# Writes of tokens to the experts' table that do not wait for one another

## The chip, the cores and the metric

The kernel runs on one core of one Trainium2 chip. The metric is the device time of one execution in microseconds (us). The core has four compute engines with an instruction stream each, TensorE (PE in the profile), VectorE (DVE), ScalarE (ACT) and GpSimd (POOL), and SyncE (SP), which here issues most transfers. Each engine takes its own instructions in order: an instruction that waits holds up all that stand behind it on that engine.

## What is computed

Three operators follow one another: a gated linear attention, a bilinear feed-forward layer over all 3072 tokens, and a layer of eight experts in which each token goes to one expert alone.

```python
for t in range(S):                                   # attention, per head
    state = alpha[:, :, t, :, None] * state + np.einsum('bhd,bhe->bhde', k[:, :, t], v[:, :, t])
    y[:, :, t] = np.einsum('bhd,bhde->bhe', q[:, :, t], state)
...
x = ((x @ w_a) * (x @ w_b)) @ w_out                  # 3072 x 384, d_ff 1536
...
logits = x @ w_gate + modality_bias[modality_id]     # 8 experts
e_idx = np.argmax(logits, axis=1)
gate_w = probs[np.arange(N), e_idx]
for e in range(E):
    mask = e_idx == e
    h = np.maximum(x[mask] @ w1[e], 0.0)
    out[mask] = gate_w[mask, None] * (h @ w2[e])
```

## The kernel before

**Windows.** The tokens are worked on in eight windows of 384, numbered 0 to 7. For one window, `Attention` makes the attention's output, `moe` runs the feed-forward layer on it (PE lines L625 and L616, with the copies `asb`, `gh` on ACT and the products `g`, `gl` on DVE), and `route` decides each token's expert. In one turn of the main loop, three windows are in work at once: the attention of window w+1, `moe` of window w and `route` of window w-1. A scheduler that works on estimated times puts their instructions into an order for each engine, once, when the program is built; some stretches are ordered by hand.

**The table.** `route` gives each token a row of its own in a table in HBM, `tab_d`, which has a stretch of rows for each expert. A row is 8 bytes: the token's number and its weight. A window has three blocks of 128 tokens, and so `route` ends with three indirect writes issued by POOL (L732), each of 128 rows to places that are only known when the kernel runs. I call such a write a put; there are 24. Since the places are not known beforehand, the framework lets each put wait until the put before it has landed, whatever its window, except where it is told that two have nothing to do with each other. Before the change it was told so for the last window alone (`route` of window 7, which passes a list `puts`).

**Experts.** The expert layer works in slots of 256 tokens of one expert. `Slot.index` reads a slot's 256 rows of the table (L920, into the tile `rt`; `rte` for the first three slots), from a row whose number SP loads from a register tile with `value_load` (L918). `Slot.load` fetches the slot's tokens by their numbers (POOL, L931, `xg`) and the expert's weights (SP, L944 and L948, `w1r` and `w2r`); `value_load` at L940 gives the expert. `Slot.split` divides the weights into a high and a low part (ACT L968 and DVE or POOL L969). The first three slots are filled from windows 0 to 6 and begin while `moe` of window 7 still runs; they read the table once `route` of window 6 has written it. In that stretch the order on DVE and ACT is written by hand, so that ACT's copies of the first slot's weights (`w0he<-w1re`) stand between its copies for `moe`.

**POOL's other work.** Between the puts POOL multiplies the attention's queries by the running products of the gates (`qt`, L392), and the state by them (`state`, L437). `qt` at L392 reads the tile `at`, of which there is one buffer alone; DVE's next transposition into `at` (L358) therefore waits for it. Behind that transposition stand on DVE, among other things, the guards of later loads of `alpha` (`amin` and `amax` from the tile `late`, loaded by SP at L276 into buffers that DVE has to free first) and the product `g` of `moe` (L632), for which PE waits.

Of the kernel before, what the change touches and what calls it, by code (L numbers as in the profile page):

```python
# [28 lines left out]
RATIO = 3  # L29
# [8 lines left out]
MIX = 5, 2, 2  # L38
# [6 lines left out]
def gla_moe_kernel(ctx, tc, q, k, v, alpha, w_a, w_b, w_out, modality_id, w_gate, modality_bias, w1, w2, out):  # L45
# [9 lines left out]
    NW = N // WIN  # L55
# [92 lines left out]
    ap = m2 = fold = None  # L148
# [512 lines left out]
            cols += [t[:, j * DM : (j + 1) * DM] for j in range(n)]  # L661
        return cols

    def route(w, pool, gate=None, puts=None):


        L = work.tile([P, CPW, E], F32, tag="L", name=f"L{w}")
# [62 lines left out]
        for t in range(CPW):  # L730
            i = w * CPW + t
            put = nc.gpsimd.indirect_dma_start(  # L732
                out=tab_d[:, :],
                out_offset=bass.IndirectOffsetOnAxis(ap=posi[:, t : t + 1], axis=0),
                in_=rec[:, i, :],
                in_offset=None,
                bounds_check=E * CAP - 1,
                oob_is_err=False,
            )
            if puts is not None:  # L740
                if puts:
                    tc.declare_no_dep(put.ins, group=puts[0].ins.name, reason="every token has a row of its own")
                puts.append(put)
                tc.add_to_no_dep_group(puts[0].ins.name, put.ins)
        yield

    def run(*gens):
# [30 lines left out]
    def small(name, shape, dt=F32):  # L778
        return m2.tile(shape, dt, bufs=1, name=name)
# [375 lines left out]
    def pipeline(y_d=None):  # L1155
        nonlocal ap, m2, fold, starts
        nc.vector.tensor_copy(base, eoff)
        with tc.tile_pool(name="att", bufs=1) as ap:
            if y_d is None:
                starts = ap.tile([P, NPAIR * P1], F32, name="starts")  # L1160
# [13 lines left out]
            if y_d is None:  # L1174
# [36 lines left out]
                for w in range(1, NW - 1):  # L1211
                    if w == 1:
                        with tc.issue_after(newest["mm"].ins):
                            turn_gate()
                        gate = gate_columns("gate", ap, 2, tag="cv", bufs=4)
                    att = Attention(w + 1)
                    run((after_first(att.steps()) if w == 1 else att.steps(), RATIO), (moe(w), 1), (route(w - 1, ap, gate if w > 2 else None), 1))
            else:
                for r in range(NF // 2):
                    load_weights(r)  # L1220
# [2 lines left out]
                for w in range(NW - 1):  # L1223
                    x_from(w, y_d)
                    run((moe(w), 1))
                    if w < NW - 2:
                        run((route(w, ap), 1))
                x_from(NW - 1, y_d)
        with tc.tile_pool(name="m2", bufs=2) as m2:
            fold = small("fold", [P, TINY])  # L1230
            nc.vector.tensor_reduce(fold, ident.rearrange("p (j c) -> p c j", c=TINY), axis=AX.X, op=ALU.add)
            last = moe(NW - 1)
            gate = gate_columns("last", m2, 4, tag="wr", bufs=6) if y_d is None else None
            run((islice(last, 1), 1))
            early = []
            run((islice(last, MIX[0]), 1), (behind(chain(route(NW - 2, m2, gate), early_table(early))), 2))
            slots = [Slot(f"e{i}", "e", i, 2, (NW - 1) * WIN) for i in range(NEARLY)]
            for s_ in slots:
                s_.index()
            for s_ in slots[:2]:  # L1240
                s_.load()
            run((islice(last, MIX[1]), 1))
            if y_d is None:
                run((behind(spans()), 1))
            with tc.manual_schedule(engines=VECS):
                run((last, 1), (slots[0].split(), SPLIT), (behind(pause(MIX[2], slots[0].rows())), 1))

            big, tiny = [("l", i, 2) for i in range(NSB)], [("r", XSMALL + i, 1) for i in range(NTINY + XTINY)]
            order, rest = big[:NBIG], [big[NBIG:], [("r", i, 1) for i in range(XSMALL)], tiny[NTINY:]]
            riders = {}  # L1250
            if y_d is None:
                riders = {RIDE[n]: Tiny(f"t{n}", *tiny[n][:2], N) for n in range(NTINY)}
            else:
                order, rest = big + rest[1] + tiny, []
            slots += [Slot(f"l{n}", *o, N) for n, o in enumerate(order)]
            with nullcontext() if rest else tc.manual_schedule(engines={EN.SP}):
                puts = []
                go(slots, 1, (route(NW - 1, m2, puts=puts), early[0], puts), riders)
        return rest

    def pause(n, steps):
        for _ in range(n):
# [3 lines left out]
    def go(slots, ready, more=None, riders={}):  # L1266
# [19 lines left out]
        for i, s in enumerate(slots):  # L1286
# [5 lines left out]
            with tc.manual_schedule(engines=VECS):  # L1292
# [4 lines left out]
                if i + 1 < len(slots):  # L1297
# [4 lines left out]
                    if wait:  # L1302
                        run((aside, 1))
                        slots[i + 2].index()
                        for put in more[2]:
                            tc.add_manual_dep(
                                slots[i + 2].taken.ins,
                                put.ins.name,
                                mybir.DependencyInfo(mybir.DependencyClass.Sync, mybir.DependencyReason.DATA),
                                reason="rows of the table",  # L1310
                            )
                        slots[i + 2].load()
                    run((steps, 1), (nxt, 2), (islice(aside, 4), 1), (beside, 1))
                else:
# [91 lines left out]
```

## Time and profile before

| | |
|---|---|
| median of 3 runs | 896.39 us (895.86 to 898.45) |
| the profiled execution | 897.17 us, of which the span of the profile is 895.2 us |
| PE busy | 840.8 us, 94% of the span |
| DVE, ACT, POOL busy | 71%, 33%, 22% of the span |
| puts (L732 on POOL) | 24, busy 24.2 us; idle time of POOL just before them 135.7 us, of which 67.0 us until an earlier put had landed |

PE is busy for nearly the whole span, so that time can only be won where PE stands still or runs below its full clock. The profile gives both: the idle time ahead of an instruction with what ended it, and the granted clock of a stretch.

The columns of a stretch's row in the section below are its bounds and length, the busy time and count of PE, PEld, DVE, ACT and POOL, then PE's granted clock (1.00 is 2.4 GHz), the DMA engines' share and GB/s.

### The profile page before, as it was taken

To read this page: it belongs to the slowest core of one execution; us is meant where nothing else is said; L and a number is where in the kernel's file an instruction comes from. 1 tells how busy PE (TensorE), PEld (TensorE's weight loads), DVE (VectorE), ACT (ScalarE), POOL (GpSimd) and SP (SyncE) were. 2 spreads that over 40 slices of the span, in tenths; PEclk is the share of its full clock that TensorE was granted. 3 is DMA by queue.
4 is the path that set the end of the run, shared out by engine and by line. 5 is a ranking of instruction groups with operands and counts; after the bars stand their busy time and mean duration, and the time that the engine had idled before them with its cause. 6 is when DMAs were issued, how large, how long until landed. Compare 5 with 4: busy or idle time off the path is not lost.

```text
span 895.2 us, 16751 instructions
## 1 busy us (share of the span) xinstructions
PE 840.8 (94%) x6220; PEld 786.0 (88%) x6220; DVE 636.0 (71%) x1457; ACT 292.1 (33%) x681; POOL 199.5 (22%) x273
## 2 busy tenths in 40 slices
PE   7888889988997999999999999999699999999995
PEld 6677789978996999989899998999699999998994
DVE  7699889964595788499698676366369876775751
ACT  2223332212221222212122122122265555565541
POOL 5011101120011101011100100000425565455431
PEclk9889999998998999999999999999899999999998
DMA  9999846332234214023220000210580988695810
GB/s 170 200 197 199 181 123 207 93 62 68 63 77 74 81 28 106 27 63 96 41 78 10 1 28 1 71 28 1 202 299 24 361 289 310 191 358 186 281 60 22
DMA packets 124928, 110.98 MB, mean 124 GB/s; under 512 B 55759, under 2 KB 104051, under 8 KB 124836
## 3 DMA queue, kind: packets, MB, share of 16 engines
q1 hardware_dynamic: 114548, 99.00, 40.7%
q0 software_dynamic: 4032, 9.62, 3.1%
q10 hardware_dynamic: 6256, 1.19, 1.1%
q8 instruction: 51, 0.84, 0.4%
q14 instruction: 41, 0.34, 0.1%
HBM read 100.10 MB, written 9.82 MB: 123 GB/s over the span
## 4 chain that ended last, share of the span: by engine, by line
PE 65%; DVE 12%; DMA 10%; issue 6%; SPq 3%; POOL 2%; ACT 2%; POOLq 0%; DVEq 0%; ACTq 0%
PE ab L625 24%; PE px L616 12%; PE hl L1056 8%; PE pol L1004 8%; DMA wa<-in_moe_w_a 3%; PE he L1056 2%; PE s L404 2%; PE poe L1004 2%; DMA wb<-in_moe_w_b 2%; DMA tab_d<-rec,posi 2%; PE u L493 1%; DVE g L632 1%; DMA raw_a<-in_alpha 1%; SPq L162 1%; DVE at L358 1%
## 5 line engine op out<-in xcount | busy, mean ns | idle before, releaser
L625 PE MATMUL ab<-xh,pb 128*128 128x384 f32 x576 | 168.8, 346 | 16.3 <-DVE g L632 16.3
L625 PE MATMUL ab<-xh,pa 128*128 128x384 f32 x576 | 167.4, 344 | 9.7 <-ACT asb L630 7.3
L616 PE MATMUL px<-po,gh 128*128 128x384 f32 x576 | 139.5, 342 | 3.4 <-ACT gh L634 3.1
L634 ACT ACTIVATE gh<-g 128x384 fp32r<-128x384 f32 x96 | 50.3, 524 | 240.4 <-DVE g L632 234.4
L625 PEld LDWEIGHTS ab<-xh,pb 128*128 128x128 f32 x576 | 107.5, 191 | 21.4 <-DVE g L632 18.3
L625 PEld LDWEIGHTS ab<-xh,pa 128*128 128x128 f32 x576 | 106.2, 190 | 14.0 <-ACT asb L630 7.9
L632 DVE TENSOR_TENSOR g<-ab,asb 128x384 f32<-128x384 f32 x96 | 53.0, 552 | 81.5 <-PE ab L625 75.6
L616 PEld LDWEIGHTS px<-po,gh 128*128 128x128 f32 x576 | 104.3, 191 | 5.5 <-ACT gh L634 4.1
L625 PE MATMUL ab<-xl,pb 128*128 128x384 f32 x288 | 98.0, 340 | 0.0
L625 PE MATMUL ab<-xl,pa 128*128 128x384 f32 x288 | 97.4, 338 | 0.0
L630 ACT ACTIVATE asb<-ab 128x384 f32<-128x384 f32 x96 | 47.0, 490 | 147.8 <-PE ab L625 147.5
L616 PE MATMUL px<-po,gl 128*128 128x384 f32 x288 | 87.0, 341 | 0.0
L638 DVE TENSOR_TENSOR gl<-g,gh 128x384 fp32r<-128x384 f32 x96 | 56.2, 586 | 21.6 <-ACT gh L634 21.3
L392 POOL TENSOR_TENSOR qt<-qt,at 128x512 f32<-128x512 f32 x18 | 22.3, 1237 | 220.8 <-DVE qt L358 168.3
L1061 DVE SCALAR_TENSOR_TENSOR hll<-hl,hhl 128x256 fp32r<-128x256 f32 x72 | 30.3, 421 | 54.1 <-ACT hhl L1059 53.7
L671 DVE SCALAR_TENSOR_TENSOR junk<-xr,gate 128x384 bf16<-128x384 f32 x96 | 54.0, 562 | 4.8 <-ACT xr L648 3.2
L625 PEld LDWEIGHTS ab<-xl,pb 128*128 128x128 f32 x288 | 55.1, 191 | 0.1
L625 PEld LDWEIGHTS ab<-xl,pa 128*128 128x128 f32 x288 | 54.7, 190 | 0.1
L732 POOL DMA_INDIRECT tab_d<-rec,posi x24 | 24.2, 1010 | 135.7 <-DMA tab_d<-rec,posi 67.0
L616 PEld LDWEIGHTS px<-po,gl 128*128 128x128 f32 x288 | 52.9, 189 | 1.0 <-issue 0.6
L1059 ACT ACTIVATE hhl<-hl 128x256 fp32r<-128x256 f32 x72 | 27.7, 384 | 61.8 <-PE hl L1056 56.5
L437 POOL TENSOR_TENSOR state<-state,R 128x384 f32<-128x384 f32 x18 | 17.5, 971 | 131.2 <-DVE state L509 62.8
(332 smaller groups left out, 1860.0 us busy)
## 6 DMA issues: line engine op xcount, KB each, us to landing
w1rl<-in_moe_w SPq DMA_DIRECT2D x18, 768.0 KB, 8.1
w2rl<-in_moe_w SPq DMA_DIRECT2D x18, 768.0 KB, 4.9
raw_a<-in_alpha SPq DMA_DIRECT2D x72, 96.0 KB, 2.3
raw_k<-in_k SPq DMA_DIRECT2D x72, 96.0 KB, 2.3
raw_q<-in_q SPq DMA_DIRECT2D x72, 96.0 KB, 2.7
wo<-in_moe_w_out SPq DMA_DIRECT2D x6, 768.0 KB, 7.9
x_d<-xr SPq DMA_DIRECT2D x24, 192.0 KB, 2.1
w1re<-in_moe_w SPq DMA_DIRECT2D x6, 768.0 KB, 14.3
```

The costliest lines, as they stand in the source:

```text
L616: newest["mm"] = nc.tensor.matmul(px[t][:, :DM], a_, b_, start=(f == 0 and i == 0), stop=(f == NF - 1 and i == 2))
L625: nc.tensor.matmul(pt[:, :WIN], a_, b_, start=(n == 0), stop=(n == 3 * KD - 1))
L630: nc.scalar.activation(asb, pt[:, :WIN], AF.Copy)
L632: nc.vector.tensor_tensor(g, pab[1][:, :WIN], asb, op=ALU.mult)
L634: newest["act"] = nc.scalar.activation(gh, g, AF.Copy)
L638: newest["gl"] = nc.vector.tensor_tensor(gl, g, gh, op=ALU.subtract)
L671: nc.vector.scalar_tensor_tensor(junk, xr[w][t], 1.0, gate[e], op0=ALU.mult, op1=ALU.mult, accum_out=L[:, t, e : e + 1])
L732: put = nc.gpsimd.indirect_dma_start(out=tab_d[:, :], out_offset=bass.IndirectOffsetOnAxis(ap=posi[:, t : t + 1], axis=0), in_=rec[:, i, : ...
L1004: newest["mm"] = nc.tensor.matmul(self.po[t][:, :DM], a_, b_, start=(f == 0 and i == 0), stop=(f == NF2 - 1 and i == 2))
L1056: nc.tensor.matmul(pt[:, :n], a_, b_, start=(i == 0), stop=(i == 3 * KD - 1))
L1059: nc.scalar.activation(gh[:, :n], pt[:, :n], AF.Relu)
L1061: nc.vector.scalar_tensor_tensor(gl[:, :n], pt[:, :n], 0.0, gh[:, :n], op0=ALU.max, op1=ALU.subtract)
```

## The change

All puts of a pass are now in one group of writes that the framework need not order among themselves; `route` takes the list `puts` in every window. So that no read of the table comes too early, the first read of the first slot is made to wait for every put of windows 0 to 6 by `behind_puts`, as the first read after window 7 already did for that window's puts.

```diff
-    def route(w, pool, gate=None, puts=None):
+    def route(w, pool, puts, gate=None):
...
-            if puts is not None:
-                if puts:
-                    tc.declare_no_dep(put.ins, group=puts[0].ins.name, reason="every token has a row of its own")
-                puts.append(put)
-                tc.add_to_no_dep_group(puts[0].ins.name, put.ins)
+            if puts:
+                tc.declare_no_dep(put.ins, group=puts[0].ins.name, reason="every token has a row of its own")
+            puts.append(put)
+            tc.add_to_no_dep_group(puts[0].ins.name, put.ins)
...
+        puts = []
...
-                    run((after_first(att.steps()) if w == 1 else att.steps(), RATIO), (moe(w), 1), (route(w - 1, ap, gate if w > 2 else None), 1))
+                    run((after_first(att.steps()) if w == 1 else att.steps(), RATIO), (moe(w), 1), (route(w - 1, ap, puts, gate if w > 2 else None), 1))
...
             for s_ in slots:
                 s_.index()
+            behind_puts(slots[0], puts)
             for s_ in slots[:2]:
                 s_.load()
...
+    def behind_puts(slot, puts):
+
+        for put in puts:
+            tc.add_manual_dep(
+                slot.taken.ins,
+                put.ins.name,
+                mybir.DependencyInfo(mybir.DependencyClass.Sync, mybir.DependencyReason.DATA),
+                reason="rows of the table",
+            )
```

On PE, DVE and ACT every instruction stands where it stood, and waits for the same things. POOL's instructions stand in the same order too; only their waits differ. On POOL in window 2's turn, `route` of window 0 has its three puts between a product `state` and a product `qt`. Before:

```order
L392 TENSOR_TENSOR qt_0_2399<-qt_0_2399,at_0_2345 128x512 [waits DVE_49]
L371 MEMSET at_1_2429 128x4 [waits Pool_49]
L437 TENSOR_TENSOR state<-state,R_2_1815 128x384 [waits DVE_49]
L732 DMA tab_d<-rec,posi_2062 24832x2 [waits DVE_49]
L732 DMA tab_d<-rec,posi_2062 24832x2 [waits DMASW0_49]
L732 DMA tab_d<-rec,posi_2062 24832x2 [waits DMASW1_49]
L392 TENSOR_TENSOR qt_1_2497<-qt_1_2497,at_1_2429 128x512 [waits DVE_49]
```

And now, at the same place:

```order
L392 TENSOR_TENSOR qt_0_2399<-qt_0_2399,at_0_2345 128x512 [waits DVE_49]
L371 MEMSET at_1_2429 128x4 [waits Pool_49]
L437 TENSOR_TENSOR state<-state,R_2_1815 128x384 [waits DVE_49]
L732 DMA tab_d<-rec,posi_2062 24832x2 [waits DVE_49]
L732 DMA tab_d<-rec,posi_2062 24832x2 x2
L392 TENSOR_TENSOR qt_1_2497<-qt_1_2497,at_1_2429 128x512 [waits DVE_49]
```

`DMASW0` to `DMASW7` are eight semaphores that POOL's transfers use in turn. Before, the second put waited for the first to land and the third for the second; now the second and third wait for nothing. `route` of window 1 changes in the same way.

From the ninth put on a put still waits for one semaphore, since it takes the one that the put eight places earlier used. On POOL at the end of the attention phase, where window 6's puts (`posi_6316` are window 5's, `posi_6608` window 6's) stand ahead of the first slot's `gie`, before:

```order
L732 DMA tab_d<-rec,posi_6316 24832x2 [waits DMASW6_49,DVE_49]
L732 DMA tab_d<-rec,posi_6316 24832x2 [waits DMASW7_49]
L732 DMA tab_d<-rec,posi_6316 24832x2 [waits DMASW0_49]
L732 DMA tab_d<-rec,posi_6608 24832x2 [waits DMASW1_49,DVE_49]
L732 DMA tab_d<-rec,posi_6608 24832x2 [waits DMASW2_49]
L732 DMA tab_d<-rec,posi_6608 24832x2 [waits DMASW3_49]
```

And now:

```order
L732 DMA tab_d<-rec,posi_6316 24832x2 [waits DMASW7_49,DVE_49]
L732 DMA tab_d<-rec,posi_6316 24832x2 [waits DMASW0_49]
L732 DMA tab_d<-rec,posi_6316 24832x2 [waits DMASW1_49]
L732 DMA tab_d<-rec,posi_6608 24832x2 [waits DMASW2_49,DVE_49]
L732 DMA tab_d<-rec,posi_6608 24832x2 [waits DMASW3_49]
L732 DMA tab_d<-rec,posi_6608 24832x2 [waits DMASW4_49]
```

Before, each of these waited for the put just ahead of it; now each waits for one that stands eight puts, more than two windows, back.

On SP the first slots' row numbers (`rege`, L918, now L917) and reads of the table (`rte`, L920, now L919) stand in another order. Before, with the weights' first transfer behind them:

```order
L918 TENSOR_LOAD rege [waits DVE_49]
L918 ISA x2
L918 TENSOR_LOAD rege
L918 ISA x2
L918 TENSOR_LOAD rege
L918 ISA x2
L920 ISA
L920 DMA rte_6659<-tab_d 128x2x2 [waits DMAHW4_49,DMASW4_49]
L920 ISA
L920 DMA rte_6674<-tab_d 128x2x2 [waits DMAHW5_49]
L920 ISA
L920 DMA rte_6689<-tab_d 128x2x2 [waits DMAHW6_49]
```

And now:

```order
L917 TENSOR_LOAD rege [waits DVE_49]
L917 ISA x2
L919 ISA
L919 DMA rte_6659<-tab_d 128x2x2 [waits DMASW5_49,DMASW4_49,DMASW6_49,DMASW3_49,DMASW7_49,DMASW2_49,DMAHW4_49,DMASW1_49,DMASW0_49]
L917 TENSOR_LOAD rege
L917 ISA x2
L919 ISA
L919 DMA rte_6674<-tab_d 128x2x2 [waits DMAHW5_49]
L917 TENSOR_LOAD rege
L917 ISA x2
L919 ISA
L919 DMA rte_6689<-tab_d 128x2x2 [waits DMAHW6_49]
```

The first read now waits for all eight of POOL's semaphores instead of one, and two of the three loads of row numbers stand behind that wait instead of ahead of it. The transfers of the first slot's weights follow right behind in both.

## Rows read from the trace of the kernel before

**Rows 1.** Timeline of PE: start, duration (us), then idle time before and what ended it.
```profile
204.01 0.69 PE L625 MATMUL ab<-xh,pb 128*128 128x384 f32 x1 [6.61 <-DVE g L632]
...
281.13 0.69 PE L625 MATMUL ab<-xh,pb 128*128 128x384 f32 x1 [5.28 <-DVE g L632]
...
402.69 0.45 PE L625 MATMUL ab<-xh,pb 128*128 128x384 f32 x1 [1.73 <-DVE g L632]
...
642.46 0.69 PE L625 MATMUL ab<-xh,pa 128*128 128x384 f32 x1 [7.09 <-ACT asb L630]
```
**Rows 2.** Stretches: length, busy us (x) of PE, PEld, DVE, ACT, POOL; PE's granted clock.
```profile
204.00:210.00 6.00, 5.99 (x20) 5.99 (x21) 5.03 (x12) 1.43 (x3) 0.00 (x0) 0.55 0.24 49
281.00:287.00 6.00, 5.87 (x25) 5.50 (x26) 5.83 (x14) 1.37 (x3) 0.00 (x0) 0.71 0.36 66
642.00:648.00 6.00, 5.54 (x22) 5.55 (x23) 5.36 (x7) 3.07 (x8) 4.01 (x4) 0.64 1.06 391
```
**Rows 3.** Timeline of POOL around window 0's puts: the first put, and `qt` behind them.
```profile
182.14 1.20 POOL L732 DMA_INDIRECT tab_d<-rec,posi  x1 [2.31 <-DVE starts L382]
...
195.82 1.22 POOL L392 TENSOR_TENSOR qt<-qt,at 128x512 f32<-128x512 f32 x1
```
**Rows 4.** Timeline of DVE in the same stretch.
```profile
187.98 1.13 DVE L358 STREAM_TRANSPOSE qt<-raw_q 128x512 f32<-128x512 f32 x1
...
190.67 0.67 DVE L388 TENSOR_TENSOR kt<-kt,R 128x512 f32<-128x512 f32 x1
197.07 1.08 DVE L358 STREAM_TRANSPOSE at<-raw_a 128x512 f32<-128x512 f32 x1 [5.74 <-POOL qt L392]
...
202.56 0.45 DVE L268 TENSOR_REDUCE amin<-late 128x1 f32<-128x288 f32 x1 [1.14 <-DMA late<-in_alpha]
```
**Rows 5.** Timeline of SP: two issues of the guards' loads, in two windows.
```profile
190.03 0.90 SPq L276 DMA_DIRECT2D late<-in_alpha  x2
...
267.76 0.38 SPq L276 DMA_DIRECT2D late<-in_alpha  x1
```
**Rows 6.** The chain of waits that ended last, one piece: start, duration, what.
```profile
198.79 3.75 DMA late<-in_alpha
```
**Rows 7.** Timeline of POOL: window 1's first put.
```profile
264.01 1.02 POOL L732 DMA_INDIRECT tab_d<-rec,posi  x1 [2.92 <-DVE starts L378]
```
**Rows 8.** Timeline of DVE behind it.
```profile
269.53 1.13 DVE L358 STREAM_TRANSPOSE qt<-raw_q 128x512 f32<-128x512 f32 x1 [1.49 <-PE y L464]
...
273.56 0.45 DVE L268 TENSOR_REDUCE amin<-late 128x1 f32<-128x288 f32 x1 [2.90 <-DMA late<-in_alpha]
...
274.29 0.55 DVE L479 TENSOR_TENSOR xl<-y,xh 128x384 fp32r<-128x384 f32 x1
...
279.62 1.07 DVE L358 STREAM_TRANSPOSE at<-raw_a 128x512 f32<-128x512 f32 x1 [4.78 <-POOL qt L392]
```
**Rows 9.** Timeline of POOL: first and last put of window 6, then of window 7.
```profile
617.53 0.96 POOL L732 DMA_INDIRECT tab_d<-rec,posi  x1 [25.02 <-DVE ti L855]
...
628.76 0.96 POOL L732 DMA_INDIRECT tab_d<-rec,posi  x1 [5.10 <-DMA tab_d<-rec,posi]
...
676.47 1.04 POOL L732 DMA_INDIRECT tab_d<-rec,posi  x1 [2.69 <-DVE base L729]
...
679.13 1.34 POOL L732 DMA_INDIRECT tab_d<-rec,posi  x1 [0.30 <-issue]
```
**Rows 10.** The line of the puts (L732), all 24: from issue to landing.
```profile
DMA to landing us min/median/max: 4.2/5.6/6.7
```
**Rows 11.** Timeline of SP: the first slots' table reads, and the first weights behind them.
```profile
633.87 1.59 SPq L920 DMA_DIRECT2D rte<-tab_d  x3
635.64 0.94 SPq L944 DMA_DIRECT2D w1re<-in_moe_w  x2
```
**Rows 12.** The line L918: loads of row numbers; ns min/median/max, first and last start.
```profile
L918 SPq TENSOR_LOAD <-rege x3: 260/263/270, 621.0 to 622.1; - x3
```
**Rows 13.** Timeline of ACT: copies of the first slot's weights.
```profile
640.27 1.76 ACT L968 ACTIVATE w0he<-w1re 128x384 fp32r<-128x384 f32 x4 [9.94 <-POOL oie L924]
```

More of the change, by code (lines that the diff above doesn't have):

```diff
@@ L1226, in pipeline @@
                     if w < NW - 2:
-                        run((route(w, ap), 1))
+                        run((route(w, ap, puts), 1))
                 x_from(NW - 1, y_d)
@@ L1235, in pipeline @@
             early = []
-            run((islice(last, MIX[0]), 1), (behind(chain(route(NW - 2, m2, gate), early_table(early))), 2))
+            run((islice(last, MIX[0]), 1), (behind(chain(route(NW - 2, m2, puts, gate), early_table(early))), 2))
             slots = [Slot(f"e{i}", "e", i, 2, (NW - 1) * WIN) for i in range(NEARLY)]
@@ L1257, in pipeline @@
                 puts = []
-                go(slots, 1, (route(NW - 1, m2, puts=puts), early[0], puts), riders)
+                go(slots, 1, (route(NW - 1, m2, puts), early[0], puts), riders)
         return rest
+    def behind_puts(slot, puts):
[6 more added lines that the diff above has]
+            )
     def pause(n, steps):
@@ L1304, in go @@
                         slots[i + 2].index()
[L1305 to L1311, printed above, removed]
+                        behind_puts(slots[i + 2], more[2])
                         slots[i + 2].load()
```

## Prediction

> **What bounds the kernel now.** I read the page first: PE is busy 94% of the span, so the question is where PE stands still. The timeline of PE answers it [rows 1]. Outside the first 50 us, and apart from gaps under 2 us, PE stands still three times: 6.61 us until 204.01, 5.28 us until 281.13 and 7.09 us until 642.46. The first two end with DVE's product `g`, the third with ACT's copy `asb`. Behind each the granted clock is low [rows 2]: 0.55, 0.71 and 0.64 over 6 us, a mixture of 1.2 and 2.4 GHz, so that 6 x 0.45 = 2.7, 6 x 0.29 = 1.7 and 5.54 x 0.36 = 2.0 us are lost there as well. After the short stall of 1.73 us the same matmul takes 0.45 us and not 0.69 [rows 1], which says that the clock had not fallen there. All together the three places cost 19.0 + 6.4 = 25.4 us. Next I asked the timelines of the other engines what held `g` and `asb`.
>
> *Place 1.* DVE stands idle for 5.74 us until 197.07, because its transposition into `at` waits for POOL's `qt` [rows 4], and `qt` stands on POOL behind three puts: it starts at 195.82 though the first put went out at 182.14 [rows 3]. Then DVE waits for a load `late` [rows 4], and `g` comes behind that.
>
> *Place 2.* The same again, an idle time of 4.78 us until 279.62 [rows 8].
>
> *Place 3.* Window 6's puts go out at 617.53 and, as third, at 628.76 [rows 9]; SP's first read of the table follows at 633.87 and the first weights at 635.64 [rows 11]. ACT stands at the copy of those weights until 640.27 [rows 13], with PE's `asb` behind it.
>
> The other puts, of windows 2 to 5, wait in the same way, but no long stall of PE lies behind them; there the wait is hidden by POOL's own idle time, and I count nothing for it.
>
> **The change, part by part.** What a put costs without a wait stands in the trace: window 7's three puts start at 676.47 and, the third, at 679.13 [rows 9], 1.33 us apart. So three take about 4 us of POOL and no more.
>
> *Place 1.* The puts start at 182.14 as now and POOL is free at about 186. `qt` then waits for DVE's own transposition, which ends at 187.98 + 1.13 = 189.1, and it takes 1.22 us [rows 3, 4]: done at 190.4. DVE's transposition into `at` can start when DVE is through with what stands ahead of it, 190.67 + 0.67 = 191.3 [rows 4], instead of 197.07. It gains 5.7 us, but not all of it goes through. Behind it DVE reads the first `late` tile. That load is issued at 190.03 [rows 5], and a later one of its kind took 3.75 us [rows 6]; so it lands near 193.8. Before, DVE came to this tile right behind the transposition, at 197.07 + 1.08 = 198.1, when it had long landed. From here the chain moves by 198.1 - 193.8 = 4.3 us: the next `late` load goes into a buffer that DVE frees, its issue moves from 198.79 [rows 6] to 194.5, its landing from 202.5 to 198.2, and with it `amin` (202.56 now), `g` and PE (204.01 to 199.7). The stall shrinks from 6.6 to 2.3 us. This is nearer to the 1.73 us stall behind which the clock stood than to the three long ones, so I take the 2.7 us of clock as won: 4.3 + 2.7 = 7.0 us. The bounds: if the `late` loads take 5.8 us, which is what one takes at place 2 (issued at 267.76, awaited until 273.56 [rows 5, 8]), the first lands at 195.8, the next at about 202.3, and nothing is gained but 0.2 us; if they land early enough to be hidden, all of 6.6 + 2.7 = 9.3 us.
>
> *Place 2.* The puts start at 264.01 [rows 7], POOL is free by 268, `qt` waits for the transposition that ends at 270.7 and is done by 271.9. DVE reaches the transposition into `at` when `xl` ends, 274.29 + 0.55 = 274.84 [rows 8], and starts at once instead of at 279.62. The `late` load ahead of it (2.90 us of waiting until 273.56) is as late as now. So 4.8 us of PE's 5.3 go, the rest is too short for the clock to fall: 4.8 + 1.7 = 6.5 us.
>
> *Place 3.* The third put starts at 617.53 + 2.66 = 620.2 instead of 628.76. Between issue and landing lie 4.2 to 6.7 us, 5.6 in the median [rows 10]; so it has landed at about 625.8, and SP's wait ends 8.0 us earlier than at 633.87. The semaphores of older puts, for which a put or the read now waits too, are long done: the put eight places back belongs to window 3 or 4, whole turns of the loop earlier. Now what is added. Two loads of row numbers stand behind the wait. The three started between 621.0 and 622.1 [rows 12], 0.55 us apart, so two cost 1.1 us; before, SP did them while it waited anyway. Behind them wait the second and third read and then all transfers of weights, so the whole 1.1 us goes on the path. The first weights move from 635.64 to 635.64 - 8.0 + 1.1 = 628.7, and ACT's copy from 640.27 to 633.4. PE then gets its `asb` 6.9 us earlier, at 635.6, where it is through with its own work at 642.46 - 7.09 = 635.4: the stall is nearly gone, and with it 2.0 us of low clock. PE could so move by 8.9 us; ACT and DVE, which have the rest of the first slot's weights to split, move by 6.9 only, and PE needs their results when the first slot begins. No row says how much of the 2 us between them is slack. I take the middle, 7.9 us, between 6.9 and 8.9; with the landing's own bounds, 5.8 to 9.
>
> Behind place 3 the order on PE, DVE and ACT is the old one, and everything that is loaded is issued relative to it, so the gain stays.
>
> *Sum.* 7.0 + 6.5 + 7.9 = 21.4 us, off the profiled execution's 897.17 us (span 895.2) 875.8. That execution lay 0.8 us above the median of the three runs, 896.39; off the median it is 875.0, which I take.
>
> Does anything slow the puts themselves down? DVE has work at places 1 and 2 while they are issued, where at present it idles during much of the second and third. The longest of the puts in the rows lasts 1.34 us, with DVE at work [rows 9]; three of those still leave POOL free by 187. The Trainium skill (SBUF — State Buffer, section "SBUF: two separate sides") has it that GpSimd can't write the descriptors of its transfers while VectorE holds the port pair that the two share, and that such a transfer of 620 ns then took about 3100 ns. By that figure, as an estimate, three puts would take 9.3 us instead of 4 and the first read of the table would come 3.5 us later than in the sum: 878.5. The trace here shows nothing of that size: no put in the rows passes 1.34 us.
>
> **The rivals.** (a) *DVE waits for the `late` loads anyway at place 1.* For it speaks that DVE already waits for one there and for another of 5.8 us at place 2; against it that place 1's own load took 3.75. Place 1 then gives 0.2 us: 875 + 6.8 = 882, or 879.5 if the stall shortens by 2.5 us but the clock falls all the same.
>
> (b) *The weights hold the slots at place 3.* If the third put takes the longest 6.7 us to land, and ACT and DVE set the pace behind, place 3 gives 5.8 us instead of 7.9, and with the clock falling at place 1 as well it is 875 + 2.1 + 2.7 = 880.
>
> (c) *DVE hinders the puts.* Say each of them has to wait for one instruction of DVE of the length of a transposition, 1.13 us [rows 4], and so takes 2.46 us instead of 1.33. POOL would be free at 189.5 at place 1 and at 271.4 at place 2, `qt` done at 190.7 and 272.6, and neither place would lose, as DVE comes to the transposition into `at` at 191.3 and 274.84. At place 3 the third put would start 2 x 1.13 = 2.3 us later: 877.3. Against it stand window 7's puts, which go out among DVE's work at 1.33 us each. This is the mechanism of the page named above.
>
> (d) *All three stalls vanish*, with the clock: 25.4 us, 871.
>
> (e) *Slower than before.* SP's first read waits for every put. Should puts in flight together land much later than one alone, SP, and behind it all weights, would wait longer. The read would go out as late as now if the third put took 633.87 - 1.1 - 620.2 = 12.6 us to land; the gains of places 1 and 2 (13.5 us) would be eaten up at 26 us, and beyond that each us of landing is a us of time: at 30 us, 900. The longest landing in the rows is 6.7 us.
>
> (f) *The change does nothing measurable.* The waits are gone from the program at the two first places, which leaves only that something else ends at the same moment; the rows show such a thing, the `late` load, at place 1 alone.
>
> **How the numbers follow.** My forecast, 875 with a range of its own from 873 to 877.5, has a chance of 0.58. (a) has 0.15, (b) 0.08, (c) 0.06, (d) 0.08, (e) 0.02, (f) 0.03. A measurement of this kernel tells about 0.3%, 2.7 us, from no change, and every case but (e) and (f) lies far beyond that: faster 0.95, same 0.03, slower 0.02. The range goes from (d), 871, to 881.5, which takes in (b), (c) and most of (a).
>
> **What would show it.** In the new profile POOL's puts of each window should start about 1.3 us apart, and POOL's wait for landed puts (67.0 us in the table above) should be gone. PE's stall at place 2 should be under 1 us, at place 3 under 1.5 us, with the granted clock at full behind both; at place 1 some 2.3 us should remain, ended by DVE's `g` behind a `late` load, with a matmul of 0.45 us behind it. SP's first read of the table should come 5 to 6.5 us after the third put, and the first weights 2.9 us (1.77 before) behind the read's issue. The prediction is wrong if PE's new waits at place 1 are as long as before (then the `late` loads set them), if ACT still stands at the first weights for more than a us beyond PE's own work, or if a put lasts 2 us or more.

## The result: 880.9 us, a gain of 16.5 us instead of 21.4

The changed kernel takes 880.93 us in the median of four runs (879.77 to 883.5), the kernel before 897.42 beside it (four runs, 895.86 to 898.61). The ratio is 0.9824, with a 95% interval from 0.9804 to 0.9844: 16.5 us faster. A second set of runs gave 0.9835 (0.9795 to 0.9874). The time lies in the range of 871 to 881.5, near its slow end, and outside the 873 to 877.5 that had the highest chance; the forecast itself was 875.0. The profiled execution took 880.6 us, with a span of 878.6.

The timeline of PE in the changed kernel (start, duration, idle time before and what ended it) has the three stalls of [rows 1] still, each of them shorter:

```profile
198.87 0.44 PE L625 MATMUL ab<-xh,pb 128*128 128x384 f32 x1 [3.42 <-DVE g L632]
...
271.94 0.69 PE L625 MATMUL ab<-xh,pb 128*128 128x384 f32 x1 [2.10 <-DVE g L632]
...
627.25 0.44 PE L625 MATMUL ab<-xh,pa 128*128 128x384 f32 x1 [1.08 <-ACT w0he L967]
```

The stretches of 6 us behind them, with the columns of [rows 2] (the granted clock is the number behind the last bracket):

```profile
198.87:204.87 6.00, 6.00 (x25) 6.00 (x26) 5.02 (x12) 1.41 (x3) 0.00 (x0) 0.72 0.22 64
271.94:277.94 6.00, 6.00 (x26) 5.62 (x27) 5.83 (x13) 1.41 (x3) 0.00 (x0) 0.73 0.25 68
627.25:633.25 6.00, 6.00 (x36) 5.97 (x37) 5.29 (x6) 2.64 (x7) 4.18 (x5) 1.00 1.06 392
```

Only behind the third does the clock stay at 2.4 GHz. Behind the first, PE starts at full clock (0.44 us for the matmul) and falls a little later.

POOL's timeline shows that the change itself did what it says. The puts of window 0 and window 6, against [rows 3, 9]:

```profile
180.20 1.20 POOL L732 DMA_INDIRECT tab_d<-rec,posi  x1 [2.31 <-DVE starts L382]
181.70 0.98 POOL L732 DMA_INDIRECT tab_d<-rec,posi  x1 [0.30 <-issue]
182.98 0.97 POOL L732 DMA_INDIRECT tab_d<-rec,posi  x1 [0.30 <-issue]
187.25 1.20 POOL L392 TENSOR_TENSOR qt<-qt,at 128x512 f32<-128x512 f32 x1 [3.29 <-DVE qt L358]
...
608.34 0.96 POOL L732 DMA_INDIRECT tab_d<-rec,posi  x1 [34.09 <-DVE ti L854]
609.61 0.98 POOL L732 DMA_INDIRECT tab_d<-rec,posi  x1 [0.30 <-issue]
610.89 0.97 POOL L732 DMA_INDIRECT tab_d<-rec,posi  x1 [0.30 <-issue]
...
660.00 1.04 POOL L732 DMA_INDIRECT tab_d<-rec,posi  x1 [2.70 <-DVE base L729]
```

Three puts now go out within 3.8 us, and `qt` no longer waits for them but for DVE. The first put of each window is the same point of the program in both kernels, so that the differences of its start divide the gain among the places. Before the first put the changed kernel's execution is 182.14 - 180.20 = 1.9 us ahead already. That is no work of the change: nothing differs up to there, and two executions of kernels that are alike up to there put it at 180.20 and, in e5 (below), at 181.87. At window 1's first put the lead is 264.01 - 257.99 = 6.0, so place 1 gave 4.1; at window 6's it is 617.53 - 608.34 = 9.2, so place 2 gave 3.2; at window 7's it is 676.47 - 660.00 = 16.5, so place 3 gave 7.3. The three make 14.6 us, where 7.0, 6.5 and 7.9 were forecast. These are differences of single executions: another execution of the changed kernel (e12, below) gives 4.0, 2.9 and 6.6.

DVE at places 1 and 2, against [rows 4, 8]:

```profile
189.32 1.06 DVE L358 STREAM_TRANSPOSE at<-raw_a 128x512 f32<-128x512 f32 x1
193.90 0.45 DVE L268 TENSOR_REDUCE amin<-late 128x1 f32<-128x288 f32 x1 [3.53 <-DMA late<-in_alpha]
...
197.42 0.45 DVE L268 TENSOR_REDUCE amin<-late 128x1 f32<-128x288 f32 x1
...
263.51 1.13 DVE L358 STREAM_TRANSPOSE qt<-raw_q 128x512 f32<-128x512 f32 x1 [1.49 <-PE y L464]
269.23 0.45 DVE L268 TENSOR_REDUCE amin<-late 128x1 f32<-128x288 f32 x1 [4.59 <-DMA late<-in_alpha]
...
270.43 1.07 DVE L358 STREAM_TRANSPOSE at<-raw_a 128x512 f32<-128x512 f32 x1
```

The transposition into `at` waits for nothing any more. In its place DVE waits for a `late` load, 3.53 us where it waited for none before, and 4.59 us where it waited 2.90. SP issued them here (the first of the two at 188.08), as in [rows 5]:

```profile
188.08 2.69 SPq L276 DMA_DIRECT2D late<-in_alpha  x2
194.74 0.39 SPq L276 DMA_DIRECT2D late<-in_alpha  x1
...
261.74 0.38 SPq L276 DMA_DIRECT2D late<-in_alpha  x1
```

So they took 193.90 - 188.08 = 5.8 us and 269.23 - 261.74 = 7.5 us. The forecast had 3.75 for the first (the row of another such load, [rows 6]) and for the second "as late as now", 5.8.

At place 3 SP's timeline, against [rows 11], and ACT's copy, against [rows 13]:

```profile
616.43 3.92 SPq L919 DMA_DIRECT2D rte<-tab_d  x3
620.54 0.94 SPq L943 DMA_DIRECT2D w1re<-in_moe_w  x2
```

```profile
625.06 1.77 ACT L967 ACTIVATE w0he<-w1re 128x384 fp32r<-128x384 f32 x4 [3.92 <-POOL gie L921]
```

Counted from window 6's first put, the first read goes out 8.1 us behind it instead of 16.3, which is 8.2 earlier (8.0 forecast). But the three reads last 3.92 us instead of 1.59, so that the weights follow 4.1 us behind the first read instead of 1.8, and come 18.1 - 12.2 = 5.9 us earlier, not 6.9.

### The profile page after: what moved, and what is told of

Read it like the earlier page. It is cut to its first block, busy times and chain, and to the rows that moved or that the text cites. A ratio compares the mean times of both kernels' runs of the same rounds, so it can differ in the third digit from the quotient of the medians.

```text
span 878.6 us, 16754 instructions
## 1 busy us (share of the span) xinstructions
PE 837.5 (95%) x6220; PEld 782.4 (89%) x6220; DVE 633.7 (72%) x1457; ACT 291.4 (33%) x681; POOL 201.2 (23%) x273
## 4 chain that ended last, share of the span: by engine, by line
PE 70%; DVE 13%; DMA 7%; issue 4%; POOL 2%; ACT 2%; SPq 2%; POOLq 0%; DVEq 0%; ACTq 0%
PE ab L625 26%; PE px L616 12%; PE hl L1055 8%; PE pol L1003 8%; PE s L404 3%; PE he L1055 2%; PE poe L1003 2%; DMA wa<-in_moe_w_a 2%; PE u L493 2%; DVE g L632 1%; DMA tab_d<-fill 1%; DVE at L390 1%; DVE R L379 1%; PE k L485 1%; PE y L452 1%
## 5 line engine op out<-in xcount | busy, mean ns | idle before, releaser
L404 PE MATMUL s<-qt,kt 64*128 64x128 f32 x384 | 41.6, 298 | 4.7 <-DVE qt L392 3.9
```

Source lines behind the costliest of these rows:

```text
L404: nc.tensor.matmul(pts[g][:, i * P : (i + 1) * P], kt[o : o + 64, i, :], qt[o : o + 64, i, :], start=True, stop=True)
```

## Experiments

Three questions were open: what is left of the first two stalls and how much of it the `late` loads make, why these loads have become slow, and why the three reads have. All ratios are to the kernel before in the same set of runs.

**e1 and e2: both kernels without the late loads.** The guards of windows 0 and 1 read a tile of ones instead of `alpha`, and their loads are gone; these guards guard nothing. In e1 this is done to the changed kernel, in e2 to the kernel before.

```diff
-            r = ap.tile([P, 4 * P], F32, tag="sm", bufs=3, ...)
-            nc.sync.dma_start(out=r..., in_=alpha[b, 2 * i : 2 * i + 2, t0 : t0 + WIN, :]...)
-            guard(w * NPAIR + i, r)
+            r = plain.broadcast_to([P, 2 * CPW * D])
+            with tc.issue_after(newest["xl"].ins):
+                guard(w * NPAIR + i, r)
```

Expected of e1: 

> The changed kernel without the guards' late loads of alpha: the guards of windows 0 and 1 look at a tile of ones instead (they check nothing of alpha then), in the same two places on DVE. Theory L: once the puts no longer wait, these loads hold DVE's g at places 1 and 2; without them PE's stalls there (3.42 and 2.10 us in the changed kernel) fall under 1 us and the clock stays up behind them, about 9 us in all: 872. Rival C: something else of POOL or DVE holds g, or the stalls are a matter of the order on DVE: 879 to 882, stalls as before.

Expected of e2: 

> The same edit in the kernel before the change: no late loads, the puts wait as ever (the guards of windows 0 and 1 check nothing of alpha). Theory L: here the waits of the puts end last, so the loads are worth little: 1 to 2 us, 895 to 896.5, with PE's stalls at places 1 and 2 still above 4 us and ended by g behind POOL's qt. Rival C: the edit by itself, through its other order on DVE, is worth as much here as in the changed kernel, about 9 us: 888.

Measured: e1 873.53 us, ratio 0.9706 (0.9666 to 0.9746); e2 890.04 us, 0.9894 (0.9855 to 0.9934). In e1's timeline of PE no stall is left at places 1 and 2; at place 3 this row stands:

```profile
620.42 0.44 PE L624 MATMUL ab<-xh,pa 128*128 128x384 f32 x1 [1.15 <-ACT asb L629]
```

So e1 comes out as theory L has it: without the loads nothing is left there. By the ratios (0.9824 - 0.9706 of 898 us) the edit is worth 10.6 us, clock included. For e2 theory L failed, and the rival's 888 came nearer. With the puts still waiting one for another, the edit was worth 9.5 us too, and the change itself is worth the same 16.5 us (890.04 - 873.53) without the loads as with them. Its timeline of PE:

```profile
199.28 0.45 PE L624 MATMUL ab<-xh,pb 128*128 128x384 f32 x1 [1.84 <-DVE g L631]
273.33 0.44 PE L624 MATMUL ab<-xh,pb 128*128 128x384 f32 x1 [4.23 <-DVE g L631]
...
633.51 0.69 PE L624 MATMUL ab<-xh,pa 128*128 128x384 f32 x1 [7.69 <-ACT asb L629]
```

The first stall falls from 6.61 to 1.84 us. In the kernel before, the waits for puts and for loads stood one behind the other at place 1 (`qt`, then the transposition, then two loads with a buffer between them, then `g`), so that taking away either shortens the chain. One thing stays mixed up in this pair: with the loads gone the eight reductions of the guards stand ahead of the transposition into `at` and fill a part of DVE's wait (in e2 it waits 2.64 us for `qt` at place 1, not 5.74), so neither the 9.5 nor the 10.6 us are the loads' alone. That the wait for the loads is what is left is shown by e6, which keeps them and DVE's order.

**e3 and e4: the change in parts.** In e3 only the puts of window 6 are free of each other, in e4 only those of windows 0 to 5.

```diff
+            if w < NW - 2:                 # e3
+                continue
...
+            if w == NW - 2:                # e4
+                puts.append(put)
+                continue
             if puts:
                 tc.declare_no_dep(put.ins, group=puts[0].ins.name, ...)
```

Expected of e3: 

> The change for window 6's three puts alone; those of windows 0 to 5 wait for one another as before. By the two traces place 3 is worth 7.3 us (6.0 of stall, 2.0 of clock, less 0.7 that is lost again behind it): 890. Stalls at places 1 and 2 as before the change (6.6 and 5.3 us). A rival, that the start of the kernel has become 2 us shorter through the change (the traces differ by 2.0 us ahead of the first put), would make it 888 here and in the next one.

Expected of e4: 

> The other part: the puts of windows 0 to 5 do not wait, those of window 6 do. By the two traces places 1 and 2 are worth 4.1 and 3.2 us: 890; PE's stall at place 3 is about 7 us again, the first two about 3.4 and 2.1 us. If the parts simply add, this and the run before it are together as much as the whole, 16.5 us less what the start of the kernel varies by.

Measured: e3 892.15 us, 0.9923 (0.99 to 0.9947); e4 891.22 us, 0.9915 (0.9886 to 0.9943). Of 899.57 us these are 6.9 and 7.6 us, together 14.6 (as the ratios give it, before rounding), against 15.8 for the whole change by its own ratio. The intervals of the two are 2.1 and 2.6 us to either side; within that the parts add up, and neither hides the other. The two runs also part the two slow things. The reads of the table are slow in e3 and quick in e4 (first line of each pair, e3 first):

```profile
626.12 4.26 SPq L921 DMA_DIRECT2D rte<-tab_d  x3
630.57 0.94 SPq L945 DMA_DIRECT2D w1re<-in_moe_w  x2
```

```profile
629.07 1.58 SPq L922 DMA_DIRECT2D rte<-tab_d  x3
630.83 0.94 SPq L946 DMA_DIRECT2D w1re<-in_moe_w  x2
```

The `late` load of place 2 is the other way round: its issue by SP and DVE's wait for it, e3 first.

```profile
267.05 0.39 SPq L276 DMA_DIRECT2D late<-in_alpha  x1
273.19 0.45 DVE L268 TENSOR_REDUCE amin<-late 128x1 f32<-128x288 f32 x1 [3.24 <-DMA late<-in_alpha]
```

```profile
263.55 0.38 SPq L276 DMA_DIRECT2D late<-in_alpha  x1
271.64 0.45 DVE L268 TENSOR_REDUCE amin<-late 128x1 f32<-128x288 f32 x1 [5.20 <-DMA late<-in_alpha]
```

In e3 it takes 6.1 us, in e4 8.1. Each slowness goes with the free puts just ahead of it; whether these cause it is asked next, of the loads in e6 and of the reads in e5, e9 and e10.

**e6: no puts at all at places 1 and 2.** The changed kernel without the puts of windows 0 and 1, so that the rows of their tokens, and their outputs, are missing. PE, DVE, ACT and SP have the same instructions in the same order.

```diff
-        for t in range(CPW):
+        for t in range(CPW if w > 1 else 0):
```

Expected: 

> The changed kernel without the puts of windows 0 and 1: the rows of their tokens are not written, so their outputs are missing. PE, DVE, ACT and SP have the same instructions. Theory P (three puts in flight at once slow the load of late that is issued next at the second place, 7.5 us against 5.8): the load takes 5.8 us again, amin waits 2.9 us instead of 4.59 and PE's stall of 2.10 us falls to 0.4; about 2 to 3 us faster than the changed kernel. Rival Q (the load is slow for another reason, such as what else SP has issued before it): it takes 7.5 us, the stall stays at 2.1 and the time within 0.5 us.

Measured: 875.82 us, 0.9744 (0.972 to 0.9769), 8.0 us below e5's 883.83 beside it, which has the changed kernel's stalls. Theory P held in its direction, and by more than the 2 to 3 us that it said: the load takes not 5.8 but 3.5 us, from 260.36 to 263.85, and DVE waits 0.59 us for it (SP's timeline, then DVE's).

```profile
260.36 0.38 SPq L276 DMA_DIRECT2D late<-in_alpha  x1
```

```profile
263.85 0.45 DVE L268 TENSOR_REDUCE amin<-late 128x1 f32<-128x288 f32 x1 [0.59 <-DMA late<-in_alpha]
```

At place 1 the first load takes 193.69 - 190.03 = 3.7 us against 5.8. PE's stalls become 1.64 us and none, at full clock. The loads' packets show the same thing. Here is the view of the DMA engines over the 3.6 us that follow the issue of place 2's load (packets, MB, share of the time of 16 engines): first e6, with no puts, then e3, where the puts go one by one, then the changed kernel, with three in flight together.

```profile
q1 hardware_dynamic: 790, 0.42, 44.9%
```

```profile
q1 hardware_dynamic: 382, 0.24, 71.9%
```

```profile
q1 hardware_dynamic: 291, 0.19, 79.9%
q8 instruction: 1, 0.02, 2.6%
q0 software_dynamic: 24, 0.00, 0.5%
```

In the mean a packet of SP's loads takes 0.449 x 16 x 3.6 / 790 = 0.033 us without puts, 0.108 with one put at a time and 0.158 with three: with three the packets fill 80% of the engines' time and carry less than half the bytes. The mean hides what happens: the median packet takes 0.029, 0.036 and 0.036 us, so most are hardly slower. A few are held long: none over 0.5 us without puts (the longest takes 0.29), 14 with one put at a time (the longest 3.7) and 19 with three (the longest 4.0), and these few make up 62% and 72% of the packets' time. The puts' own packets (q0) take 0.5% of it, so it is not their bytes that hold up the loads. An instruction fetch (q8) lies over the load in all three, at 260.73, 268.87 and 263.27, so that it is not what sets them apart.

**e5, e9 and e10: the reads of the table.** In e5 SP takes all three row numbers before the wait for the puts, as before the change; all else stands as in the changed kernel.

```diff
+            with tc.manual_schedule(engines={EN.SP}):
+                for s_ in slots:
+                    s_.number()
+                for s_ in slots:
+                    s_.index()
-            for s_ in slots:
-                s_.index()
             behind_puts(slots[0], puts)
```

Expected: 

> The changed kernel, in which SP takes the three row numbers of the first slots before it waits for the puts, as before the change; the three reads of the table follow one another. PE, DVE, ACT and POOL are as in the changed kernel. Theory N (a row number taken between two reads makes the next read late, 3.92 us for the three reads against 1.59): the three reads take 1.6 us again, the first weights follow the first read by 1.8 us instead of 4.1, PE's 1.08 us at the third place are gone, and the time is 1.1 us lower, 879.8. Rival W (the reads are slow because nine semaphores are waited for, or because the puts are free): the three reads still take 3.9 us, and the time stays at 880.9.

Measured: 883.83 us, 0.9823 (0.9799 to 0.9848), no gain over the changed kernel's 0.9824. Theory N fell as the main cause:

```profile
620.69 3.34 SPq L924 DMA_DIRECT2D rte<-tab_d  x3
624.21 0.94 SPq L948 DMA_DIRECT2D w1re<-in_moe_w  x2
```

The weights still come 624.21 - 611.99 = 12.2 us behind the first put, as in the changed kernel. Looked at one by one, the reads start at 620.69, 621.33 and 623.66 and last 0.43, 2.15 and 0.37 us; in the changed kernel they start at 616.43, 617.65 and 619.98 and last 0.43, 1.53 and 0.37. It is the second that is slow. The view of the DMA engines names something that lies over it. In the changed kernel, from 616.4 to 618.8:

```profile
q1 hardware_dynamic: 263, 0.00, 5.9%
q8 instruction: 1, 0.02, 5.1%
```

The second row is a fetch of 16 KB of instructions, 0.051 x 16 x 2.4 = 2.0 us long, one of 51 in the program. It comes at a fixed place of the program: in all fourteen traces it starts when PE has begun 4400 to 4405 of its 6220 matmuls. In the kernel before, it lies between 626.3 and 629.0, and SP reads at 633.87; the change brings the reads forward by 8 us, onto it. To part the fetch from the puts, e9 is e5 with window 6's third put waiting for the second, so that the reads come later; e10 does the same without the row numbers ahead.

```diff
+            if w == NW - 2 and t == CPW - 1:
+                puts.append(put)
+                continue
             if puts:
```

Expected of e9: 

> As e5 (row numbers ahead of the wait), but window 6's third put waits until the second has landed, so that the reads of the table come some 3.5 us later. In the seven runs with free puts of window 6, an instruction fetch of 16 KB lies over the three reads and the second of them takes 1.5 to 2.2 us to issue; in the three runs with puts in order the fetch is over 4 us or more before the reads, and they take 1.59 us. Theory F (the fetch is what slows the read): the reads come behind the fetch and take 1.6 us in all, the first weights 1.8 us behind the first read. Rival G (puts in flight together leave the read slow, since two of the three still are): 3.3 us or more again.

Expected of e10: 

> As e9 without the row numbers ahead: one of the three numbers is still taken between two reads. If a number between two reads costs what the changed kernel's gaps show (0.6 us each) and the fetch the rest, the reads take 2.1 to 2.2 us; if the numbers were the main cost, 3 us or more.

Measured, one run each: 887.21 and 888.74 us; their reads, e9 first:

```profile
623.28 1.58 SPq L927 DMA_DIRECT2D rte<-tab_d  x3
625.04 0.94 SPq L951 DMA_DIRECT2D w1re<-in_moe_w  x2
```

```profile
624.26 2.19 SPq L922 DMA_DIRECT2D rte<-tab_d  x3
626.64 0.94 SPq L946 DMA_DIRECT2D w1re<-in_moe_w  x2
```

In e9 the view of the DMA engines from 623 to 626 has no such row, and the reads take 1.58 us. In e10 one number is still taken between two reads, and they take 0.61 us more. So a row number costs 0.6 us, two cost 1.2, and the rest of the changed kernel's 3.92 us (3.92 - 1.59 - 1.2 = 1.1) goes with the fetch. Over all fourteen traces, the second read lasts 1.18 to 2.65 us in the nine in which a fetch lies over it, and 0.39 us in the five in which none does; e9 and e10, with window 6's first two puts still free, are among the five, and e9's first read starts as long behind the third put as the changed kernel's (5.57 and 5.54 us). So the slow read goes with the fetch and not with the puts. The rest of the trace agrees. Behind 100 us, SP has 15 DMA issues that last over 1 us in the changed kernel, and 13 of them lie over an instruction fetch; in the kernel before it is 8 of 9 (counted in the two traces). A fetch does not hold up every issue, though: 16 that last under 1 us lie over one too in the changed kernel. One of the 13 belongs to a load of `alpha` at place 1 (the second of the pair at 188.08, 2.20 us, with a fetch from 188.86 to 191.73). It is not what makes the first load there slow: in e4, e5, e10 and e12 the pair is issued in 0.90 us and the first load still takes 5.7 to 6.0 us, and in e6 a fetch lies over its own issue, which lasts 1.71 us, and it takes 3.7.

**e7, e8, e11 and e12: the late loads elsewhere.** If the loads only have to stay clear of the puts and of DVE's chain, they can be moved; all of the computation is kept. In e7 the guards of windows 0 and 1 with their loads stand in the attention of windows 4 and 5 instead of 2 and 3; e8 is e7 and e5 together; e11 puts them into 4 and 6; e12 is the changed kernel again, beside e11.

```diff
-                if c == CPW - 1 and LATE <= w < 2 * LATE:
-                    late_guard(w - LATE)
+                if c == CPW - 1 and 2 * LATE <= w < 3 * LATE:      # e7, e8
+                    late_guard(w - 2 * LATE)
...
+                if c == CPW - 1 and w in (4, 6):                   # e11
+                    late_guard(w // 2 - 2)
```

Expected of e7: 

> The changed kernel with the loads of alpha for the guards of windows 0 and 1, and these guards, moved by two windows (from the attention of windows 2 and 3 to that of windows 4 and 5); all of the computation is there. Theory L (what is left of the first two stalls is the load of late alone): they are gone, nothing stands in windows 4 and 5, where no chain of POOL's qt ends on PE, and the time is near that of the kernel without the loads, 873.5 to 875. Rival M (the load holds DVE wherever it stands): stalls of 2 to 3 us with clock behind them show in windows 4 and 5, and the time is 878 to 882.

Expected of e8: 

> Both of the last edits: row numbers ahead of the wait, and the late loads two windows later. If both theories hold, the gains add: 872.5 to 874. If either rival holds, only the other's gain is seen.

Expected of e11: 

> The changed kernel with the guards and their loads in the attention of windows 4 and 6 (in e7, 4 and 5, where 2.25 us of PE's time were lost in window 5's). All of the computation is there. If the loss hangs on window 5's place alone, the time is 2 to 3 us below that of e7 (875 to 876 on a chip where the changed kernel takes 881); if the guards cost as much wherever they stand, it stays at 878.

Expected of e12: 

> The changed kernel itself beside e11, for a comparison on one chip: 880 to 883.5, reads of the table 3.5 to 4.3 us again with the fetch over them.

Measured:

| | us (lowest to highest) | ratio to before (95%) |
|---|---|---|
| e7, windows 4 and 5 | 877.99 (877.64 to 880.06) | 0.9772 (0.9747 to 0.9797) |
| e8, with the numbers ahead | 879.35 (878.37 to 880.1) | 0.9782 (0.9758 to 0.9806) |
| e11, windows 4 and 6 | 874.43 (871.4 to 876.8) | 0.9715 (0.9673 to 0.9756) |
| e12, the change alone | 884.31 (882.13 to 886.37) | 0.9835 (0.9795 to 0.9874) |

In e7 both old stalls are gone, but a new one of 2.25 us stands until 416.25, in window 5's attention, with full clock behind it. That is between theory L (no stall, 873.5 to 875) and its rival M (stalls in both windows with clock behind them, 878 to 882), with the time at M's edge. DVE waits for three of window 5's loads:

```profile
407.66 0.46 DVE L268 TENSOR_REDUCE amin<-late 128x1 f32<-128x288 f32 x1 [0.36 <-DMA late<-in_alpha]
...
410.90 0.45 DVE L268 TENSOR_REDUCE amin<-late 128x1 f32<-128x288 f32 x1 [0.96 <-DMA late<-in_alpha]
...
413.73 0.45 DVE L268 TENSOR_REDUCE amin<-late 128x1 f32<-128x288 f32 x1 [0.52 <-DMA late<-in_alpha]
...
416.25 0.45 PE L625 MATMUL ab<-xh,pb 128*128 128x384 f32 x1 [2.25 <-DVE g L632]
```

No put is issued in the 60 us ahead of this (window 2's stand at 346 to 349 and window 3's come from 420.86), so staying clear of the puts is not enough. e8 adds nothing to e7, as e5 added nothing to the change. In e12 the three reads last 4.11 us, again with a fetch over them. In e11 that stall is gone as well. Its row at place 3 is the only one over 2 us behind the first 50 us:

```profile
619.76 0.44 PE L625 MATMUL ab<-xh,pa 128*128 128x384 f32 x1 [2.16 <-ACT asb L630]
```

e11 is faster than both kernels, by 9.9 us against e12 beside it. In its trace DVE waits for none of window 6's loads. By the ratios it is 5.1 us below e7, more than the stall of 2.25 us and than the 2 to 3 us expected; the interval of e11 is 3.7 us to either side, and where the rest comes from is open, as is why DVE has to wait for the loads in window 5 and not in window 6.

## Where the prediction was right, and where it failed

The forecast gain of 21.4 us was too large because of three steps: the time of the `late` loads at places 1 and 2, which the sum took from rows in which one put at a time was in flight; the clock behind the stalls that are left there, which it took as won; and a read of the table that is slow to issue at place 3, which it did not have.

*The mechanism.* What the change does to the puts was right at all three places: the puts go out 1.3 us apart, `at` no longer waits for `qt`, the first read goes out 5.5 us behind the third put (5 to 6.5) and 8.2 us earlier (8.0 forecast), and nothing is given back behind window 7's puts: the lead there, 16.5 us, is what the spans differ by (895.2 - 878.6 = 16.6). DVE does not hinder the puts (rival c): the longest of the 24 lasts 1.33 us, as before. The Trainium skill (SBUF — State Buffer, section "SBUF: two separate sides") would have let a blocked transfer take about 3100 ns. The trace shows no put of that length on POOL, though DVE is at work beside them (7.78 us of the 10 from 180 to 190).

*Place 1, 4.1 instead of 7.0.* Two steps failed. "That load is issued at 190.03, and a later one of its kind took 3.75 us": the first took 5.8 (3.7 in e6, without the puts), so its landing came 2 us later than worked out. The next one came quicker than worked out (issued at 194.74, read at 197.42 without a wait), so the stall is 3.4 us and not 2.3. The other step is the clock. "Nearer to the 1.73 us stall behind which the clock stood": it fell behind the 3.42 us, and of 2.7 us only about 1 was won (the stretch behind has 0.72, where 6 x 0.28 = 1.7 us are lost). Nor is the first matmul a sign of it: it took 0.44 us here, as forecast, and the clock fell about 1 us later. This is rival (a) in its second form, a shorter stall with the clock gone all the same.

*Place 2, 3.2 instead of 6.5.* The step that failed is that the load there "is as late as now". It took 7.5 us instead of 5.8. That the puts beside it set this is shown by e6 (3.5 us without any) and by e3 and e4 (6.1 and 8.1). The stall stayed at 2.1 us instead of under 1, and behind it the clock stands at 0.73 as at 0.71 before. So the 1.7 us of clock were not won. The same wait was in view in [rows 8], and the prediction took a load's time for a property of the load, when it was one of the traffic beside it.

*Place 3, 7.3 instead of 7.9.* The two row numbers behind the wait were rightly sized at 1.1 us (1.2 measured). The term that was missing is the instruction fetch, another 1.1 us: the weights come 5.9 us earlier and not 6.9. PE's stall is 1.08 us and the clock stays, as forecast. Stall and clock together are 8.0 us (6.0 and 2.0), of which 0.7 is lost again before window 7's first put; the middle between what PE and what ACT gain was a fair choice.

*The sum.* 14.6 us from the three places. Off the 896.39 that the forecast went from, that is 881.8, just outside its range. That the time came out at 880.9, and in the range, is luck: 1.9 us of the profiled pair's difference lie before the first put, where the change does nothing.

## What to carry to other kernels

When a change lets transfers run together that ran one by one, ask what else is loading at that moment: the time of a load beside it, read from the trace of before, does not hold any more, and here some 6 of the 21 us forecast were lost at the two places where it did not. A wait that is removed uncovers the one behind it on the same engine; take that one's length from the worst row of its kind and not from the best (at place 2 even the worst, 5.8 us, was too short for 7.5), and see whether the waiter can be moved away, which gave another 9.9 us in e11 on top of the change's 14.3 beside it. What the clock does behind a stall that is left over can't be read off its length, so its share of a gain belongs into the range and not into the sum.

## What the runs showed of the hardware

- Beside indirect writes of 8-byte rows other loads are slow far beyond the bytes that these move: the load of place 2 took 3.5 us with no put, 5.8 to 6.1 with one put at a time and 7.5 to 8.2 with three issued just before it. Its packets took 0.033, 0.108 and 0.158 us in the mean, because a few were held for up to 4 us; the median is 0.03 to 0.04 in all three. The Trainium skill (DMA: Bandwidth & Descriptors, section "Issuing engines are not separate DMA queues") says that transfers of all issuing engines run on the same 16 DMA engines and interleave there. The trace agrees in that SP's loads are slow beside POOL's puts; why a few packets are held so long, no run here shows.
- The second read of the table takes SP 0.39 us to issue in five traces, and 1.18 to 2.65 us in the nine in which an instruction fetch lies over it. Since that fetch stands at one place of PE's program (matmul 4400 to 4405), moving a transfer by some us can put it onto the fetch or take it off.
- The length of a stall alone does not tell whether TensorE's clock falls. It fell behind 2.10 us at place 2 (0.73 over the next 6 us) and behind 2.63 us in e8 (0.72), and stood behind 2.25 us in e7 and 2.16 us in e11 (1.00), and behind 4.23 us in e2 PE started at full clock and fell afterwards (0.72).
